# Last block of an SSD-and-MLP kernel: cross products one tile behind the squares, tile 14 by parts

## The chip, the cores and the metric

The kernel runs on one core of a Trainium2 chip. The metric is the device time of one execution in microseconds (us); a time of a kernel is the median of several executions.

## The reference

A selective state-space layer (mamba2's SSD) over 4 batches, 8 heads and 768 steps is followed by a two-layer perceptron with a hardswish between its layers. The output of the first, (4 x 768) tokens by 256, is the input `x` of the second:

```python
# SSD, chunk by chunk, per batch and head
y[:, :, sl] = einsum(CB * L, xc) + einsum(Cc, state) * decay_to_i
state = decay_full * state + sum_j(B_j x_j decay_from_j)
# MLP: 3072 tokens, 256 -> 2048 -> 256
h = x @ w_in
g = h * clip(h + 3, 0, 6) / 6
out = g @ w_out
```

All is in 32-bit floats. The change is in the MLP of the last block of tokens.

## The kernel before

The 768 steps are cut into six chunks of 128. Chunk k of all four batches gives one block of 512 tokens (four groups b of 128), and the MLP runs block by block. While the MLP of block k is computed, the SSD of the next chunk is woven into it. The order of instructions is written out by hand; each engine runs its own instructions in that order, and waits only for the data and buffers that it needs. The last block (k = 5) has no chunk after it.

**The first layer of a block** works on 16 tiles f of 128 hidden units by 512 tokens, each in a PSUM bank. The weights and the inputs were split into a high part, a low part and a `less` part, so that one-pass matmuls give the accuracy of 32-bit ones. `squares(k, f)` takes the tile's bank and runs four matmuls (high x high, low x low); `enlarge` scales the bank on ACT (L714); `cross` adds two more matmuls (less x less). All six are matmuls of L694, which writes `h`. `factor` then makes the hardswish: `ramp` on ACT (L733) reads `h` and writes `gT`, `times_ramp` on DVE (L738) multiplies it by `h`. After that the bank is free. In the last block four banks, `f0` to `f3`, take the tiles in turn, so tile f + 4 needs the bank of tile f.

**The second layer of the last block** is summed up in PSUM over the 16 tiles, with two running sums, `squares` (rows with `o`) and `cross` (rows with `o_less`). `split_g(k, f)` splits a tile of `gT` in the same way: the high part on ACT (L840), the low part and the `less` part on DVE (L841, L842), into buffers that four tiles share in turn. `split_out` has split `w_out` a quarter at a time (L812 on ACT, L815 and L822 on DVE), partly inside the loop of the last block. `last_out(k, f)` then runs, for each b, three one-pass products of 256 columns (L858): high, low, and `less`. Two tiles were not split: for 14 and 15 the function `whole` multiplies `gT` by `w_out` in 32 bits (L863), and each such product shows as two instructions of TensorE.

The last call of `last_out` ends the kernel: ACT scales the `squares` sums (L880), and for each b in the order 0, 2, 1, 3 come the last products, a DVE addition (L885) and the store of the result (L886) on SP's queue.

**Order around the change.** The block before (k = 4) ends with `wide_units`, with rows of L897, a DVE addition (L965) and a DVE transpose (L911). Shortly before its end, `lead` and `lead_on` run the squares of tiles 0 and 1 of the last block and enlarge them. The last block's loop goes over f = 2 to 15; in it a tile's `cross` and `factor` come two tiles behind the squares, `split_g` three behind, and `last_out` five behind.

Of the kernel before, what the change touches and what calls it, by code (L numbers as in the profile page):

```python
# [21 lines left out]
def kernel(  # L22
# [26 lines left out]
    NB, NH, S, D = x.shape  # L49
# [4 lines left out]
    NF = DF // P  # L54
# [636 lines left out]
    def part_products(k, f, n, m, start=False):  # L691
        w, y = w_parts[f // FP][n], y_parts[k][m]
        for j in range(NK):
            nc.tensor.matmul(  # L694
                out=hs_[k, f], lhsT=w[j][:, f % FP * P:(f % FP + 1) * P], rhs=y[:, j],
                start=(start and j == 0), stop=True, skip_group_check=True)

    def squares(k, f, low=True):

        pool, tag = ((ps, "f0"), (ps, "f1"), (ps, "f2"), (ps, "f3"), (ps_y, "y0"), (ps_y, "y1"))[  # L700
            f % (6 if k < NC - 1 else 4)]
        hs_[k, f] = pool.tile([P, TB], FP32, name="h", tag=tag)
        part_products(k, f, 0, 0, start=True)
        if low:
            part_products(k, f, 1, 1)

    def enlarge(k, f):

        h = hs_[k, f]
        if k < NC - 1 and (f < 2 if k == 1 else f % 4 == 3):  # L710
            nc.vector.tensor_scalar(
                out=h, in0=h, scalar1=1.0 / EPS + 1.0, scalar2=None, op0=ALU.mult)
        else:
            nc.scalar.activation(h, h, AF.Copy, scale=1.0 / EPS + 1.0)  # L714

    def cross(k, f):
        part_products(k, f, 2, 2)

    def factor(k, f):
        ramp(k, f, hs_[k, f])  # L720
        times_ramp(k, f, hs_[k, f])
# [9 lines left out]
    def ramp(k, f, h):  # L731

        nc.scalar.activation(  # L733
            gTs[k][:, f], h, AF.Relu, bias=half, scale=1.0 / 6.0)

    def times_ramp(k, f, h):
        g = gTs[k][:, f]
        nc.vector.scalar_tensor_tensor(  # L738
            out=g, in0=g, scalar=1.0, in1=h, op0=ALU.min, op1=ALU.mult)
# [89 lines left out]
    def g_homes():  # L829
        two = loads.tile([P, 2, 2, TB], F32R, name="g_pair", tag="raw", bufs=NRAW)  # L830
        ones = [pool.tile([P, 2, TB], F32R, name="g_pair", tag=tag, bufs=1)
                for pool, tag in ((const, f"w{NP - 1}"), (att, "yT"))]
        ends_["pair"] = ones + [two[:, 0], two[:, 1]]
        ends_["less"] = [pool.tile([P, TB], F32R, name="g_less", tag=tag, bufs=1)
                         for pool, tag in ((att, "bT"), (att, "csT"), (att, "bs"), (loads, "B"))]

    def split_g(k, f):
        g, pair, less = gTs[k][:, f], ends_["pair"][f % 4], ends_["less"][f % 4]
        hi, lo = pair[:, 0], pair[:, 1]
        nc.scalar.activation(hi, g, AF.Copy, scale=1.0 - EPS / 2)  # L840
        nc.vector.tensor_tensor(out=lo, in0=g, in1=hi.bitcast(FP32), op=ALU.subtract)  # L841
        nc.vector.scalar_tensor_tensor(  # L842
            out=less, in0=lo.bitcast(FP32), scalar=-1.0 / EPS, in1=hi.bitcast(FP32),
            op0=ALU.mult, op1=ALU.add)
        g_parts[f] = (hi, lo, less)

    def last_out(k, f):

        if f == 0:
            ends_["squares"] = [ps_o.tile([P, 2, DM], FP32, name="o", tag="o") for _ in range(2)]  # L850
            ends_["cross"] = [
                ps_y.tile([P, 2, DM], FP32, name="o_less", tag=f"y{u}") for u in range(2)]
            ends_["res"] = ffn.tile([P, NB, DM], FP32, name="res", tag="wide")
        o = [[ends_[n][b // 2][:, b % 2] for b in range(NB)] for n in ("squares", "cross")]

        def product(b, t, n):
            w = out_parts[t // FP][n][:, (t % FP) * DM:(t % FP + 1) * DM]
            nc.tensor.matmul(  # L858
                out=o[n // 2][b], lhsT=g_parts[t][n][:, b * P:(b + 1) * P], rhs=w,
                start=(t == 0 and b % 2 == 0 and n != 1), stop=True, skip_group_check=True)  # L860

        def whole(b, t):
            nc.tensor.matmul(  # L863
                out=o[1][b], lhsT=gTs[k][:, t, b * P:(b + 1) * P], rhs=w_out[:, t],
                start=False, stop=True, skip_group_check=True)

        if f < NF - 4:
            for b in range(NB):
                for n in range(3):
                    product(b, f, n)  # L870
            return
        for t, ns in ((f, range(2)), (f, (2,)), (NF - 2, ()), (f + 1, range(2))):
            for b in range(NB):
                for n in ns:
                    product(b, t, n)
                if not ns:
                    whole(b, t)
        res = ends_["res"]
        for u in range(2):
            nc.scalar.activation(  # L880
                res[:, 2 * u:2 * u + 2], ends_["squares"][u], AF.Copy, scale=1.0 / EPS + 1.0)
        for b in (0, 2, 1, 3):
            product(b, f + 1, 2)
            whole(b, NF - 1)
            nc.vector.tensor_tensor(out=res[:, b], in0=o[1][b], in1=res[:, b], op=ALU.add)  # L885
            nc.sync.dma_start(out=out[b * S + k * P:b * S + k * P + P, :], in_=res[:, b])  # L886
# [167 lines left out]
    for k in range(NC):  # L1054
# [53 lines left out]
            continue  # L1108
        if c == NC:
            g_homes()  # L1110
            for f in range(2, NF):
                squares(k, f)
                if f > 4:
                    last_out(k, f - 5)
                cross(k, f - 2)
                enlarge(k, f)
                factor(k, f - 2)
                if f > 2:
                    split_g(k, f - 3)
                if 3 <= f < 13:  # L1120
                    next(outs_[2 + f // 8])
            for f in (NF - 2, NF - 1):
                cross(k, f)
            factor(k, NF - 2)
            factor(k, NF - 1)
            split_g(k, NF - 3)
            for f in range(NF - 5, NF - 3):
                last_out(k, f)
            continue
        for f in range(2, NF):  # L1130
            squares(k, f)
# [95 lines left out]
```

## Time and profile before

| | |
|---|---|
| median of 3 runs | 343.51 us (343.08 to 343.96) |
| profiled execution | 343.9 us, of which 342.1 us are the span |
| TensorE (PE) | 334.7 us busy, 98% of the span |
| TensorE weight loads (PEld) | 266.1 us, 78% |
| VectorE (DVE) | 237.2 us, 69% |
| ScalarE (ACT) | 198.0 us, 58% |
| GpSimd (POOL) | 125.0 us, 37% |
| last block, from its first matmul | 293.5 us to the end |

The span goes from the first to the last instruction on the core. The busy share is an average over all stages, and overlapping matmuls count from their start to a modelled end, so the distance between starts says more than the length of a row. The chain that ended last is followed back from the last instruction, at each step to what released it. In rows, `x4` is a count of instructions, the first number is the start in us, the second the time that the group took, and a bracket names idle time before it and what ended that. The granted TensorE clock is 1.0 throughout.

### The profile page before, as it was taken

The page shows a single profiled execution, that of the slowest core. Times are in us where ns is not written, and L with a number is a line of the kernel's source. Part 1 is how long each engine was busy: PE and PEld are TensorE (multiplying, and loading weights), DVE is VectorE, ACT ScalarE, POOL GpSimd, SP SyncE. Part 2 cuts the span into 40 slices and gives each one's busy share as a digit, 9 for nine tenths or more (in the row PEclk, how much of TensorE's full clock was granted, in tenths as well). Part 3 has the DMA queues.
Part 4 walks back from the last instruction along what each step waited for, and adds up shares of the span by engine and source line. Part 5 has one row for each costly group of instructions (what it writes and reads, how often), then busy time and mean ns, then how long its engine had stood idle before and what let it go on. Part 6 is the DMA issues. An engine that isn't in the chain of part 4 may idle for free.

```text
span 342.1 us, 8181 instructions
## 1 busy us (share of the span) xinstructions
PE 334.7 (98%) x3332; PEld 266.1 (78%) x3332; DVE 237.2 (69%) x378; ACT 198.0 (58%) x415; POOL 125.0 (37%) x123
## 2 busy tenths in 40 slices
PE   6999999999999999999999999999999999999995
PEld 1664448888888888888888888888888888799994
DVE  6599999998399859565528555537476455498973
ACT  4759878757986480576460576470586030667661
POOL 3300000190284798089813089920079700000000
PEclk9999999999999999999999999999999999999999
DMA  8989968042590216166107276101160001110001
GB/s 172 175 301 192 196 216 196 2 54 75 141 136 1 60 32 147 27 85 68 24 12 154 35 90 63 23 3 17 31 77 2 2 2 17 30 17 2 1 2 61
DMA packets 89605, 25.15 MB, mean 74 GB/s; under 512 B 82208, under 2 KB 85952, under 8 KB 89056
## 3 DMA queue, kind: packets, MB, share of 16 engines
q1 hardware_dynamic: 85184, 23.33, 36.4%
q10 hardware_dynamic: 4384, 1.31, 1.8%
q8 instruction: 26, 0.43, 0.5%
q14 instruction: 11, 0.09, 0.1%
HBM read 21.33 MB, written 3.29 MB: 72 GB/s over the span
## 4 chain that ended last, share of the span: by engine, by line
PE 96%; DVE 2%; DMA 1%; ACT 0%; issue 0%; ACTq 0%
PE h L694 32%; PE wb L897 13%; PE wc L897 8%; PE o L751 8%; PE h L626 8%; PE wa L897 8%; PE o L858 4%; PE y L604 3%; PE y L503 2%; PE o_less L858 2%; PE cb L530 2%; PE y L544 1%; PE o_less L863 1%; PE d L357 1%; DMA pre<-in_a_dram 1%; PE d L493 1%
## 5 line engine op out<-in xcount | busy, mean ns | idle before, releaser
L738 DVE SCALAR_TENSOR_TENSOR gT<-gT,h 128x512 f32<-128x512 f32 x96 | 64.8, 685 | 35.9 <-ACT gT L733 34.4
L733 ACT ACTIVATE gT<-h,half 128x512 f32<-128x512 f32 x96 | 65.2, 685 | 23.9 <-PE h L694 21.9
L714 ACT ACTIVATE h<-h 128x512 f32<-128x512 f32 x66 | 38.2, 584 | 41.1 <-PE h L694 41.0
L694 PE MATMUL h<-y_hi,w_part 128*128 128x512 f32 x160 | 51.8, 408 | 0.2 <-DVE gT L738 0.2
L694 PE MATMUL h<-y_less,w_part 128*128 128x512 f32 x160 | 49.7, 397 | 0.0
L694 PE MATMUL h<-y_lo,w_part 128*128 128x512 f32 x160 | 49.5, 395 | 0.0
L797 POOL TENSOR_TENSOR s<-gT 128x512 f32<-128x512 f32 x16 | 23.8, 1489 | 46.5 <-DVE gT L738 46.5
L694 PEld LDWEIGHTS h<-y_lo,w_part 128*128 128x128 f32 x160 | 30.0, 188 | 7.4
L694 PEld LDWEIGHTS h<-y_hi,w_part 128*128 128x128 f32 x160 | 29.9, 188 | 7.2 <-DVE gT L738 0.8
L694 PEld LDWEIGHTS h<-y_less,w_part 128*128 128x128 f32 x160 | 29.3, 188 | 5.9
L385 ACT ACTIVATE L<-L,cum_n 128x64 f32<-128x64 f32 x128 | 31.6, 337 | 0.0
L751 PE MATMUL o<-w_out,gT 128*128 128x256 f32 x128 | 28.8, 381 | 0.0
L626 PE MATMUL h<-yT,w_in 128*128 128x512 f32 x64 | 27.7, 594 | 0.0
L751 PEld LDWEIGHTS o<-w_out,gT 128*128 128x128 f32 x128 | 24.1, 190 | 3.8 <-issue 0.5
L158 POOL TENSOR_SCALAR_AFFINE_SELECT L<-L 64x1024 f32<-64x1024 f32 (+1 forms) x16 | 20.3, 1276 | 11.6 <-DMA L<-cum_d 11.2
L574 DVE TENSOR_TENSOR L<-L,cb 128x512 f32<-128x512 f32 x24 | 15.2, 682 | 13.1 <-PE cb L530 13.1
L403 POOL TENSOR_TENSOR tmp<-state,eto 128x256 f32<-128x256 f32 x5 | 4.1, 817 | 54.2 <-ACT eto L389 54.1
L626 PEld LDWEIGHTS h<-yT,w_in 128*128 128x128 f32 x64 | 12.1, 190 | 14.9 <-issue 12.9
L797 POOL TENSOR_TENSOR s<-gT,s 128x512 f32<-128x512 f32 x16 | 21.3, 1338 | 0.9
L396 POOL TENSOR_TENSOR bs<-B,L 128x128 f32<-128x128 f32 x24 | 11.7, 501 | 26.9 <-ACT L L385 21.4
L797 POOL TENSOR_TENSOR gT<-gT 128x512 f32<-128x512 f32 x16 | 20.6, 1293 | 0.9
L797 POOL TENSOR_TENSOR s<-s,gT 128x512 f32<-128x512 f32 x16 | 20.5, 1287 | 0.0
(137 smaller groups left out, 594.2 us busy)
## 6 DMA issues: line engine op xcount, KB each, us to landing
raw<-in_moe_w_out_dram SPq DMA_DIRECT2D x4, 1024.0 KB
L<-cum_d SPq DMA_DIRECT2D x8, 512.0 KB
xt<-in_x_dram SPq DMA_DIRECT2D x6, 512.0 KB
raw<-in_moe_w_in_dram SPq DMA_DIRECT2D x3, 1024.0 KB
out_dram<-back SPq DMA_DIRECT2D x128, 16.0 KB
pairs<-in_C_dram SPq DMA_DIRECT2D x40, 32.0 KB
eto<-cum_e SPq DMA_DIRECT2D x20, 64.0 KB
B<-in_B_dram SPq DMA_DIRECT2D x5, 256.0 KB
```

Of the source, the lines that this page charges most:

```text
L158: nc.gpsimd.affine_select(out=t[rows], in_=t[rows], pattern=pattern, compare_op=ALU.is_ge, fill=-1e5, base=base, channel_multiplier=-1)
L385: nc.scalar.activation(Ls[c][:, b, h], Ls[c][:, b, h], AF.Exp, bias=cum_n[:, c, g:g + 1])
L574: nc.vector.tensor_tensor(out=Ls[c][:, :, hs], in0=Ls[c][:, :, hs], in1=cbs[c][q], op=ALU.mult)
L626: nc.tensor.matmul(out=h, lhsT=w_in[f // FP][:, j, f % FP * P:(f % FP + 1) * P], rhs=yTs[k][:, j].rearrange("p b i -> p (b i)"), start=(j ...
L694: nc.tensor.matmul(out=hs_[k, f], lhsT=w[j][:, f % FP * P:(f % FP + 1) * P], rhs=y[:, j], start=(start and j == 0), stop=True, skip_group_ ...
L714: nc.scalar.activation(h, h, AF.Copy, scale=1.0 / EPS + 1.0)
L733: nc.scalar.activation(gTs[k][:, f], h, AF.Relu, bias=half, scale=1.0 / 6.0)
L738: nc.vector.scalar_tensor_tensor(out=g, in0=g, scalar=1.0, in1=h, op0=ALU.min, op1=ALU.mult)
L751: nc.tensor.matmul(out=o[:, b % 2], lhsT=gTs[0][:, f, b * P:(b + 1) * P], rhs=w_out[:, f], start=(f == 0 and b % 2 == 0), stop=True, skip_ ...
L797: nc.gpsimd.tensor_tensor(out=o, in0=p_, in1=q_, op=op)
L858: nc.tensor.matmul(out=o[n // 2][b], lhsT=g_parts[t][n][:, b * P:(b + 1) * P], rhs=w, start=(t == 0 and b % 2 == 0 and n != 1), stop=True, ...
L897: nc.tensor.matmul(out=bank[:, slot], lhsT=lhs[:, j], rhs=rhs[:, j], start=(clear and j == 0), stop=True, skip_group_check=True)
```

## The change

The last block's loop gets another order. `cross` and `factor` of tiles 0 and 1 come ahead of the loop; in the loop, `cross` and `factor` come one tile behind the squares in place of two, and `split_g` two behind in place of three. The loop has one round more (f = 16), without squares, for the cross of tile 15. Tile 14 is now split like the others and multiplied by twelve one-pass products, and only tile 15 stays whole. The last call of `last_out` is for tile 13: it runs the squares products of tiles 13 and 14, then the `less` products of 13, and in its end loop the `less` product of 14 and the whole product of 15 for each b.

```diff
@@ last_out
-        if f < NF - 4:
-            for b in range(NB):
-                for n in range(3):
-                    product(b, f, n)
-            return
-        for t, ns in ((f, range(2)), (f, (2,)), (NF - 2, ()), (f + 1, range(2))):
+        for t, ns in ((f, range(3)),) if f < NF - 3 else (
+                (f, range(2)), (f + 1, range(2)), (f, (2,))):
             for b in range(NB):
                 for n in ns:
                     product(b, t, n)
-                if not ns:
-                    whole(b, t)
+        if f < NF - 3:
+            return
         res = ends_["res"]
@@ the last block
             g_homes()
-            for f in range(2, NF):
-                squares(k, f)
+            for f in range(2):
+                cross(k, f)
+                factor(k, f)
+            for f in range(2, NF + 1):
+                if f < NF:
+                    squares(k, f)
                 if f > 4:
                     last_out(k, f - 5)
-                cross(k, f - 2)
-                enlarge(k, f)
-                factor(k, f - 2)
                 if f > 2:
-                    split_g(k, f - 3)
+                    cross(k, f - 1)
+                if f < NF:
+                    enlarge(k, f)
+                if f > 2:
+                    factor(k, f - 1)
+                split_g(k, f - 2)
                 if 3 <= f < 13:
                     next(outs_[2 + f // 8])
-            for f in (NF - 2, NF - 1):
-                cross(k, f)
-            factor(k, NF - 2)
-            factor(k, NF - 1)
-            split_g(k, NF - 3)
-            for f in range(NF - 5, NF - 3):
-                last_out(k, f)
+            last_out(k, NF - 4)
+            last_out(k, NF - 3)
             continue
```

## The prediction

> **What bounds the kernel now.** I read the page first: its busy shares and its chain that ended last. Then I read that chain in order of time from 270 us on, and at two places where something other than TensorE stands in it I read the instructions by time, engine by engine.
>
> ```profile
> PE 334.7 (98%) x3332; PEld 266.1 (78%) x3332; DVE 237.2 (69%) x378; ACT 198.0 (58%) x415; POOL 125.0 (37%) x123
> PE 96%; DVE 2%; DMA 1%; ACT 0%; issue 0%; ACTq 0%
> ```
>
> TensorE is 96% of the chain, so only two things count: what work TensorE gets, and the few places where it stands still. The chain in order of time has two such places in the last block, one at its head and one at its end:
>
> ```profile
> 293.88 0.95 PE h L694 x4
> ...
> 294.92 0.41 ACT h L714
> ...
> 295.41 0.69 ACT gT L733
> ...
> 296.13 0.70 DVE gT L738
> ...
> 296.87 2.59 PE h L694 x10
> ...
> 306.64 1.40 PE h L694 x6
> 308.04 0.23 PE o L858 x2
> ...
> 309.46 1.40 PE h L694 x6
> ...
> 333.42 1.73 PE o_less L863 x8
> 335.15 0.95 PE o L858 x8
> ...
> 337.20 0.04 issue
> 337.24 0.39 PE o_less L858
> ```
>
> A tile in the steady part is six matmuls of L694 (1.40 us) and twelve products of L858: from 308.04 to 309.46, 1.42 us, so 0.118 us each. One tile is 2.82 us, and from 299 to 332 us TensorE never idles. The eight L863 instructions are four whole products (each runs as two): 1.73 us, 0.43 us a product. At the head the chain leaves TensorE for ACT and DVE. The TensorE rows of that place:
>
> ```profile
> 295.59 0.62 PE L694 MATMUL h<-y_lo,w_part 128*128 128x512 f32 x2
> 296.05 0.62 PE L694 MATMUL h<-y_less,w_part 128*128 128x512 f32 x2
> 296.87 0.73 PE L694 MATMUL h<-y_hi,w_part 128*128 128x512 f32 x2 [0.21 <-DVE gT L738]
> 297.44 0.62 PE L694 MATMUL h<-y_lo,w_part 128*128 128x512 f32 x2
> ```
>
> Pairs normally start 0.466 us apart (295.59, 296.05), so the pair at 296.87 should have started at 296.52: 0.35 us late. The next pair comes 0.57 us after it in place of 0.466, its weight load no longer running ahead: 0.10 more. The pair is tile 4's squares. With four banks it needs tile 0's bank, and that is free when the DVE step of tile 0 (L738, 296.13 to 296.82) has read it. The stall is 0.45 us.
>
> **The change, part by part.**
>
> *First two tiles' crosses ahead of all.* TensorE's order was squares 2, cross 0, squares 3, cross 1, squares 4; it becomes cross 0, cross 1, squares 2, squares 3, cross 2, squares 4. Cross 0 and 1 need only their enlargement, which ACT ran at 291.73 for 1.07 us, so until 292.80; the block begins at 293.53. Cross 0 starts there (a first pair takes 0.66 us, as now), and its ramp on ACT follows at about 294.4 and ends at 295.1. On DVE the new step stands behind the previous block's L965 and its transpose L911 (294.38, 0.71 us), so tile 0's L738 runs from 295.1 to 295.8. Squares 4 reach TensorE at 296.99. The bank is free 1.2 us ahead, and the 0.45 us go.
>
> What comes late next is cross 2, due at 296.52. Its enlargement stands behind two ramps on ACT now. Ramp 1 starts at 295.0 and ACT can take the next at 295.5. Squares 2, 0.466 us ahead of where squares 3 stood, end so that the enlargement starts at 295.79 (now tile 3's starts 1.13 us after its squares begin: 296.25 after 295.12) and ends at 296.37. With 0.04 us of handing on it makes 296.52, but the load, which normally leads by 0.23 us, starts about 0.1 us late. Between nothing and 0.1 us; I take 0.02, since the load led by only 0.10 when it had to (297.44 after 296.87). If the ramps pushed it further, the whole 0.45 us could return here. Cross 3 needs an enlargement that ends by 297.4 and is due at 297.92; cross 4, behind the two weight splits of L812 on ACT, one by 300.3 against 300.7.
>
> *Crosses one tile behind.* No instruction is added by this, and the six L694 matmuls of a step still follow each other (cross, then the next squares). Cross f-1 needs an enlargement from a step earlier, 2.82 us before. ACT's three instructions of a tile hold it 1.7 us (304.32 to 306.02; 2.7 in the two steps with L812), DVE's four at most 2.76; both were so before. Buffers of a split tile are reused four tiles on, and their last reader stays one whole step ahead. Cost: nothing, covered by a full step; without that cover each late cross would cost what it is late. No DMA is moved: the final stores stay where they are on SP's queue, and POOL does nothing here.
>
> *Fourteenth's cross at the end, fifteenth by parts.* (Counted as in the code, tiles 13 and 14.) Removed: four whole products of tile 14, 1.73 us. Added: twelve products, 12 x 0.118 = 1.42 us. Both are on the path: -0.31 us. Also added are one ACT step (L840, 0.63) and two DVE steps (L841, L842, 0.69 each) for tile 14, off the path if in time. To see that, set zero at the start of cross 14. In the trace, from the cross pair at 329.02: ramp 0.67 later, L738 at 1.40, L841 at 2.00, L842 at 2.79 to 3.48, the next L738 0.61 after a L842 starts. TensorE: cross 14 to 0.47, products of 11 to 1.89, cross 15 to 2.36, products of 12 to 3.78, squares products of 13 to 4.72, then those of 14; its first lo product is at 4.84. DVE: L842 of 13 to 3.48, L738 of 15 from 3.40, L841 of 14 from 4.00 to 4.69. That is 0.15 us ahead of its use, about what load and handing on take: between 0 and 0.1, I take 0. L842 of 14 ends at 5.48 for a use at 6.14, and tile 15's L738 at 4.09 for 6.26.
>
> *The end loop* keeps its 0.31 us stop at 337.24: b=1's product writes the tile that DVE's first L885 (336.76, 0.42 us) is still reading. The two ACT steps ahead of it now run beside tile 13's four crosses, 0.47 us more cover. That L885 waits for the whole product of b=0 too, whose second pass, at 336.28 for 0.38 us, ends at 336.66. So it can start at most 0.06 us sooner; I take 0.
>
> *A weight load for each product.* The twelve new products need twelve loads of 0.188 us; the four whole ones had eight. In the trace twelve products with twelve loads pass in 1.42 us, less than the 2.26 us of the loads alone, so they overlap. The Trainium skill, "TensorE: Matmul & The Clock Gate", Part 3, "The mechanism", says that a weight load overlaps running matmuls only where their row groups differ. All these fill the whole array, so by that rule they would not overlap. By the page's figures (an estimate: 107 ns a load, 109 ns a stream) the twelve would be 2.59 us and the sum +0.43 us; the trace's 1.42 us disagrees with the rule here.
>
> **Sum.** -0.45 + 0.02 - 0.31 = -0.74 us. The profiled execution took 343.9 us (span 342.1 and 1.8 around it), so 343.2 for such a one; it stands 0.4 above the median, and from the median of 343.51 the forecast is 342.8.
>
> **The rivals.**
> 1. *The stall moves to cross 2* (or tile 14's lo product): the ramps or L738 hold ACT or DVE longer than reckoned, the 0.45 us return, -0.31 remains: 343.2. For it: slacks of 0.1 us; one L842 in this block came 0.46 us late without any effect. Against: the durations are steady within 0.01. 0.18.
> 2. *The end loop's stop goes too.* The waits view gives the first L885's 1.7 us of idling to ACT's L880. Were ACT the true holder and L885 free 0.31 us earlier: -1.05, 342.5. Against: the matmul's end at 336.66. 0.06.
> 3. *Slower: the new products don't hide their loads.* In the tail parts of two tiles alternate; if the twelve ran as load after stream, 12 x (0.118 + 0.188) = 3.67 us for 1.73, with the stall gone +1.49: 345.0. It decides from 0.182 us a product ((1.73 + 0.45) / 12) on for any loss. Against: eight such products at 335.15 took 0.95. 0.05.
> 4. The forecast: 0.71. That the change does nothing is excluded: L863 must fall from 16 instructions to 8.
>
> **How the numbers follow.** 0.3% is 1.03 us, about what a measurement of this kernel can tell from no change. The forecast of -0.74 lies inside, 0.3 short of the bound. Three runs before spread over 0.88 us, so a difference of two medians is easily 0.35 to 0.5 off: rather over two in five of the forecast's share (0.31) fall beyond the bound, the rest within. Rival 2, just at the bound, gives 0.03 to faster, rival 1 0.02; rival 3, and 0.02 of scatter, go to slower: faster 0.36, same 0.57, slower 0.07. The range takes rival 2 less 0.35 of scatter, 342.1, and rival 1 with that scatter added, 343.5.
>
> **What would show it.** In the profile after: L863 x8 and L858 x180; no DVE releaser of L694 near 296.9, squares 4 starting near 297.0 and right behind cross 2; TensorE unbroken up to the last loop, with the products of tile 14 at 0.118 us; the stop of 0.3 us ahead of b=1 still there; span near 341.4. A wait of L694 for ACT's L714 near 296.5, or of L858 for L841 in the last 6 us, would prove rival 1; a product pitch above 0.18 us in the tail rival 3. A change anywhere before 293.5 us would be outside of this reckoning.

## The result, and the profile after

The changed kernel takes 342.81 us (median of 22 runs, 341.78 to 343.40) against 343.74 us for the kernel before (22 runs, 342.68 to 345.84): a ratio of 0.9972, 95% interval 0.9961 to 0.9983. By the ratio that is 0.96 us less, between 0.58 and 1.34. A second series (the first experiment below) gave 0.9966, 0.9953 to 0.9979. The profiled execution has a span of 340.0 us, 2.1 us less than before; most of that difference is not of the change, as will be seen.

The changed kernel is four lines shorter in `last_out`, so L885 of before is L881 now, and L880 is L876. From the page, the line of busy times and the first line of the chain:

```profile
PE 332.4 (98%) x3336; PEld 265.1 (78%) x3336; DVE 238.8 (70%) x380; ACT 198.6 (58%) x416; POOL 125.0 (37%) x123
...
PE 94%; DMA 3%; DVE 1%; SPq 1%; issue 0%; DVEq 0%
```

TensorE has four instructions more: twelve products came, eight of the whole ones went. DMA has 3% of the chain in place of 1%: here the chain leads back to the loads at the start of the kernel, by another way than before. The chain in order of time, in the last block:

```profile
292.55 5.63 PE h L694 x24
298.18 0.23 PE o L858 x2
...
331.58 1.90 PE o L858 x16
333.49 0.60 PE o_less L858 x5
334.09 0.43 PE o_less L863 x2
...
335.07 0.04 issue
335.11 0.39 PE o_less L858
...
336.51 0.42 DVE res L881
```

ACT and DVE no longer stand between the matmuls at the head: there are 24 of L694 in one piece. The wait of tile 4's squares for tile 0's bank (the bank wait) is gone. The sixteen squares products of tiles 13 and 14 pass at 0.119 us each. The stop ahead of b=1 is still there, at 335.07. In the waits view of the last block, the rows of TensorE and its weight loads are these two:

```profile
PEld o_less L858 <- DVE res L881: 0.4, 1, 0.4
PEld h L694 <- ACT h L714: 0.2, 1, 0.2
```

The second is new: cross 2 waits for its enlargement. In the instructions by time, the pair at 295.17 is cross 2, and the next pair (tile 4's squares) should have started 0.466 us behind it:

```profile
295.17 0.69 PE L694 MATMUL h<-y_less,w_part 128*128 128x512 f32 x2
295.70 0.63 PE L694 MATMUL h<-y_hi,w_part 128*128 128x512 f32 x2
```

It started 0.53 us behind: 0.06 us lost, where the bank wait had cost 0.45. There is a third place, which the prediction does not have. These are the first products of tile 0, in the trace of before and then in that of after:

```profile
299.30 0.40 PE L858 MATMUL o<-v_pair,g_pair 128*128 128x256 f32 x2
299.53 0.38 PE L858 MATMUL o_less<-v_less,g_less 128*128 128x256 f32 x1
299.75 0.40 PE L858 MATMUL o<-v_pair,g_pair 128*128 128x256 f32 x2
```

```profile
298.02 0.40 PE L858 MATMUL o<-v_pair,g_pair 128*128 128x256 f32 x2
298.25 0.28 PE L858 MATMUL o_less<-v_less,g_less 128*128 128x256 f32 x1
298.37 0.40 PE L858 MATMUL o<-v_pair,g_pair 128*128 128x256 f32 x2
```

From the first o_less product to the next pair it was 0.22 us and is 0.12. Before, tile 0's last split step on DVE was this:

```profile
298.78 0.69 DVE L842 SCALAR_TENSOR_TENSOR g_less<-g_pair 128x512 fp32r<-128x512 f32 x1
```

It ended at 299.47, 0.06 us ahead of its use. The product's weight load therefore started together with the product, at 299.53; after the change it starts at 298.14, 0.11 us ahead of its product.

Two measures serve in all that follows; the variants have one trace each, and two traces of the same kernel gave blocks within 0.02 us of each other. The **block** is the time from the last block's first L694 (293.53 us before, 292.20 after) to the start of the last addition on DVE (338.65 and 336.51). It was 45.12 us and is 44.31: 0.81 us less. The **lead** is the time from the first L626 to the block's first L694: 269.99 us before, 269.90 after, so nothing changed there. The rest of the 2.1 us stands ahead of the first L626, which started at 23.54 us before and at 22.30 after.

### The profile page after: what moved, and what is told of

Read it like the earlier page. It is cut to its first block, busy times and chain, and to the rows that moved or that the text cites. A ratio compares the mean times of both kernels' runs of the same rounds, so it can differ in the third digit from the quotient of the medians.

```text
span 340.0 us, 8193 instructions
## 1 busy us (share of the span) xinstructions
PE 332.4 (98%) x3336; PEld 265.1 (78%) x3336; DVE 238.8 (70%) x380; ACT 198.6 (58%) x416; POOL 125.0 (37%) x123
## 4 chain that ended last, share of the span: by engine, by line
PE 94%; DMA 3%; DVE 1%; SPq 1%; issue 0%; DVEq 0%
PE h L694 33%; PE wb L893 13%; PE wc L893 8%; PE o L751 8%; PE h L626 8%; PE wa L893 8%; PE o L858 4%; PE y L604 3%; PE o_less L858 2%; PE y L503 2%; PE cb L530 2%; DMA raw<-in_moe_w_in_dram 2%; PE y L544 1%; DMA pairs<-in_C_dram 1%; SPq L101 1%; PE o_less L863 1%
## 5 line engine op out<-in xcount | busy, mean ns | idle before, releaser
L738 DVE SCALAR_TENSOR_TENSOR gT<-gT,h 128x512 f32<-128x512 f32 x96 | 64.8, 685 | 33.7 <-ACT gT L733 32.2
L733 ACT ACTIVATE gT<-h,half 128x512 f32<-128x512 f32 x96 | 65.1, 684 | 25.7 <-PE h L694 23.7
L714 ACT ACTIVATE h<-h 128x512 f32<-128x512 f32 x66 | 38.2, 585 | 39.0 <-PE h L694 38.7
L694 PE MATMUL h<-y_hi,w_part 128*128 128x512 f32 x160 | 51.5, 407 | 0.0
L694 PE MATMUL h<-y_less,w_part 128*128 128x512 f32 x160 | 50.1, 399 | 0.0
L694 PE MATMUL h<-y_lo,w_part 128*128 128x512 f32 x160 | 49.5, 395 | 0.0
L694 PEld LDWEIGHTS h<-y_lo,w_part 128*128 128x128 f32 x160 | 30.0, 188 | 7.4
L694 PEld LDWEIGHTS h<-y_hi,w_part 128*128 128x128 f32 x160 | 30.0, 188 | 6.7 <-DVE gT L738 0.2
L694 PEld LDWEIGHTS h<-y_less,w_part 128*128 128x128 f32 x160 | 29.2, 188 | 6.0 <-ACT h L714 0.2
L626 PE MATMUL h<-yT,w_in 128*128 128x512 f32 x64 | 27.7, 594 | 0.0
L626 PEld LDWEIGHTS h<-yT,w_in 128*128 128x128 f32 x64 | 12.1, 190 | 14.9 <-issue 13.2
L858 PE MATMUL o<-v_pair,g_pair 128*128 128x256 f32 x120 | 21.1, 281 | 0.0
```

The source lines that it names most:

```text
L626: nc.tensor.matmul(out=h, lhsT=w_in[f // FP][:, j, f % FP * P:(f % FP + 1) * P], rhs=yTs[k][:, j].rearrange("p b i -> p (b i)"), start=(j ...
L694: nc.tensor.matmul(out=hs_[k, f], lhsT=w[j][:, f % FP * P:(f % FP + 1) * P], rhs=y[:, j], start=(start and j == 0), stop=True, skip_group_ ...
L733: nc.scalar.activation(gTs[k][:, f], h, AF.Relu, bias=half, scale=1.0 / 6.0)
L738: nc.vector.scalar_tensor_tensor(out=g, in0=g, scalar=1.0, in1=h, op0=ALU.min, op1=ALU.mult)
L858: nc.tensor.matmul(out=o[n // 2][b], lhsT=g_parts[t][n][:, b * P:(b + 1) * P], rhs=w, start=(t == 0 and b % 2 == 0 and n != 1), stop=True, ...
```

## The experiments

Each was timed in alternation with the kernel before; the ratio is against that.

**The changed kernel again** (no edit).

> The changed kernel once more. Theory: the change acts only in the last block, by three amounts: the bank stall at its head goes (0.45 us, of which a late cross 2 gives 0.06 back), the wait of the first o_less product for tile 0's L842 goes (0.10), and the tail has 0.31 us less TensorE work; in all 0.80 us less, ratio about 0.9977. The first matmul of the last block starts somewhere between 292 and 294 us, as in any run of either kernel, since the loads at the start end at different times. Rival: the block's start 1.33 us earlier in the first profile belongs to the change: then the block starts near 292.2 us here and in every variant that has the new order, and the ratio is near 0.994.

Measured: ratio 0.9966 (0.9953 to 0.9979). Block 44.33 us, 0.79 less than before. The block starts at 292.63, the first L626 at 22.61. Over the twelve traces of this study the first L626 starts anywhere from 22.30 to 24.61 us, and the lead is 269.8 to 270.1 us in all of them. The latest starts (24.61 and 23.68) belong to variants with the new order, and two variants with the old one, but for two early crosses, started at 22.57 and 22.82. So the 1.24 us at the start are not of the change. Two things vary there. The matmuls of L316 shortly ahead of it start at 17.66 to 17.97 us in ten traces; in the two whose chain begins with the load `pre` (before, and one late) they start at 18.90 and 19.25. And in eight traces TensorE stops for 0.32 to 1.24 us inside the matmuls of L604. The profile names no releaser for that stop, and its cause stays open.

**The kernel before again**, for its trace.

> The kernel before once more, for its trace. Theory: the block is 45.12 us long again, with the same three stops (0.45 us ahead of tile 4's squares, 0.10 ahead of the first o_less product, 0.31 ahead of b=1), and starts somewhere between 292 and 294 us, as far behind the first L626 (269.9 us) as in every other run. Rival: the block's start near 293.5 us belongs to this kernel.

Measured: block 45.10 us, with the bank wait at 296.94 as at 296.87 the first time. The block starts at 293.60, the first L626 at 23.52; on these two traces alone the rival would stand, and it falls by the variants' starts named above. The two equal starts came about in different ways: here the stop inside L604 took 1.14 us, and the first time there was none. The same program against itself came out at 0.9977 (0.9953 to 1.0002): the timing scatters by nearly as much as the whole effect. That is why the block in the traces, which repeats within 0.02 us, has to carry the detail.

**Order only:** the new loop, tile 14 whole as before.

```diff
-                split_g(k, f - 2)
+                if f < NF:
+                    split_g(k, f - 2)
...
-            last_out(k, NF - 4)
-            last_out(k, NF - 3)
+            last_out(k, NF - 4)      # last_out as before the change
```

> The new order (first two crosses ahead, cross one tile behind), but tile 14 multiplied whole as before. Theory: the head's 0.39 and 0.10 us are gained, the tail's 0.31 is not: 0.49 us less than before, ratio 0.9986, and L863 still 16 instructions. From the last block's first L694 to the first L885 of the end, 0.5 us less than in the first profile of before. Rival (the tail makes the gain): no difference, ratio 1.000.

Measured: ratio 0.9992 (0.9976 to 1.0008), block 44.60 us, 0.52 less than before. The waits are the same two as after the change. So the order gives 0.52 us (0.49 reckoned), and the parts on top of it 0.28 (44.60 to 44.32; 0.31 reckoned). The ratio alone could not tell this from no change.

**Parts only:** the old loop, tile 14 by parts.

```diff
             split_g(k, NF - 3)
-            for f in range(NF - 5, NF - 3):
+            split_g(k, NF - 2)
+            for f in range(NF - 5, NF - 2):
                 last_out(k, f)           # last_out as changed
```

> The old order (cross two tiles behind), but tile 14 by parts at the end. Theory: without the earlier crosses the parts come too late. By the rows of before, L841 of tile 13 ends at 334.30 for a use at 333.38 (0.96 us stop) and L841 of tile 14 at 335.70 for a use at 335.29 (0.45 us stop); less 0.31 us of work this is 1.1 us slower than before, ratio 1.003, with TensorE's L858 waiting for DVE's L841 twice. Rival (the two parts of the change are independent, and the parts give 0.31 by themselves): 0.31 us faster, ratio 0.999, no such wait.

Measured: ratio 1.0030 (1.0019 to 1.0041), slower by 0.3%; block 46.37 us, 1.25 more than before. From the waits view:

```profile
PEld o L858 <- DVE g_pair L841: 0.8, 2, 0.4
PEld h L694 <- DVE gT L738: 0.6, 1, 0.6
...
PEld o_less L858 <- DVE g_less L842: 0.5, 1, 0.5
```

The two waits for L841 are at the places expected. The third line is one that I had not reckoned with: in the changed `last_out` tile 12's products run high, low and less for each b, so its first less product comes 0.7 us sooner than when all four b had their squares first. It costs 0.57 us, and since TensorE is that much later, the first wait for L841 makes it only 0.39 us late in place of 0.96. That the sum came out near the 1.1 expected is in part luck. The bank wait (second line) is still there, as in the kernel before. One half of the change alone costs more than both together gain.

**Two crosses ahead only:** all else as before.

```diff
+            for f in range(2):
+                cross(k, f)
+                factor(k, f)
             for f in range(2, NF):
...
-                cross(k, f - 2)
+                if f > 3:
+                    cross(k, f - 2)
```

(`factor` likewise.)

> Only the first two tiles' cross and factor ahead of the loop; all other crosses two tiles behind and tile 14 whole as before. Theory: the stall at the head is that of the first two tiles alone, so it goes without the closer order: 0.45 and 0.10 us less, and no late cross 2, 0.55 us less than before, ratio 0.9984, no idle time of L694 in the last block. Rival (the closer order removes the stall): the bank wait stays or moves to tile 5 or 6, ratio 1.000.

Measured: ratio 0.9993 (0.9979 to 1.0007), block 44.94 us: 0.18 less than before, not 0.55. The bank wait is gone, but the first products of tile 0 are now these:

```profile
297.93 0.40 PE L858 MATMUL o<-v_pair,g_pair 128*128 128x256 f32 x2
298.43 0.39 PE L858 MATMUL o_less<-v_less,g_less 128*128 128x256 f32 x1
```

0.50 us from pair to o_less product in place of 0.23. TensorE arrives sooner, and tile 0's split arrives no sooner: its L840 on ACT stands behind the enlargement of tile 3. Its DVE step L842 ends at 298.38, 0.05 us ahead of the product. So 0.37 us of the 0.55 are lost at the next place (0.27 late, 0.10 for the load). My theory, that the stall is one of the first two tiles alone, is wrong.

**The same, with every split one step earlier:**

```diff
-                if f > 2:
-                    split_g(k, f - 3)
+                split_g(k, f - 2)
...
-            split_g(k, NF - 3)
```

> As the kernel with only the first two crosses ahead, but every tile's split of g one step earlier (split_g two tiles behind, as in the change); crosses stay two tiles behind and tile 14 whole. There the first o_less product of the second layer still came about 0.37 us late, behind tile 0's L842, and the block was 0.18 us shorter than before. Theory: that wait is of the late split alone. Moved a step earlier it goes, and the block (from its first L694 to the last L885) is 0.55 us shorter than before, 44.57 us in place of 45.12, ratio 0.9984. Rival: the wait comes from DVE's load and needs the closer crosses: block 44.9 us, ratio 0.9993.

Measured: ratio 1.0188 (1.0175 to 1.0201), 6.5 us slower; block 51.64 us. Tile 0's products run unbroken here (298.34 to 299.77, 1.43 us), so the reading of the wait was right and the cure was wrong. ACT's instructions by time, in the steady part:

```profile
304.75 0.67 ACT L733 ACTIVATE gT<-h,half 128x512 f32<-128x512 f32 x1
307.01 0.63 ACT L840 ACTIVATE g_pair<-gT 128x512 fp32r<-128x512 f32 x1 [1.59 <-DVE gT L738]
307.55 0.58 ACT L714 ACTIVATE h<-h 128x512 f32<-128x512 f32 x1
```

The split of a tile (L840 at 307.01) now stands right behind the ramp of the same tile (L733 at 304.75), and needs the DVE step L738 that comes after that ramp. On DVE that step stands behind the previous tile's split and a step of `w_out`, and runs from 306.30 to 306.98. ACT idles 1.59 us meanwhile, and the next enlargement waits behind L840. The crosses come late by that, then the ramps and the banks: in the waits view the weight loads of L694 wait for L738 ten times, 7.0 us in all. All splits can move up only if cross and factor move up with them. That is what the closer crosses of the change allow.

**Two splits early:** the two crosses ahead as above, and of the splits only those of tiles 0 and 1 one step sooner.

```diff
-                if f > 2:
-                    split_g(k, f - 3)
+                if f != 4:
+                    split_g(k, f - 2 if f < 4 else f - 3)
```

> The kernel with only the first two crosses ahead, and of the splits of g only those of tiles 0 and 1 one step earlier; from tile 2 on three tiles behind as before. Theory: the kernel with all splits earlier lost its 6.5 us because each L840 then stood on ACT right behind the ramp whose L738 it needs, with the next enlargement behind it; tiles 0 and 1 are finished ahead of the loop and need no such wait. So the late first o_less product goes and nothing is lost later: block 44.57 us, 0.55 us less than before, ratio 0.9984. Rival: any split moved up delays an enlargement: block above 45 us.

Measured: ratio 0.9982 (0.9963 to 1.0001), block 44.81 us, 0.31 less than before, 0.24 more than expected. Tile 0's products run unbroken, and then comes this:

```profile
299.19 0.63 PE L694 MATMUL h<-y_less,w_part 128*128 128x512 f32 x2
299.82 0.73 PE L694 MATMUL h<-y_hi,w_part 128*128 128x512 f32 x2
```

The pairs are 0.63 us apart in place of 0.47, and it is 0.57 to the one after: 0.26 us lost. And the waits view names the bank again (L694 for L738, 0.4 us by the load), now tile 6's squares waiting for tile 2. With the crosses two behind, freeing the first places uncovers the next; with them one behind, only the 0.06 us of cross 2 remain.

**The end loop:** the changed kernel with the `less` products of tile 13, then with those of tiles 11, 12 and 13, moved into it.

```diff
-        for t, ns in ((f, range(3)),) if f < NF - 3 else (
-                (f, range(2)), (f + 1, range(2)), (f, (2,))):
+        late = (NF - 3,)      # second kernel: (NF - 5, NF - 4, NF - 3)
+        for t, ns in ((f, range(2 if f in late else 3)),) if f < NF - 3 else (
+                (f, range(2)), (f + 1, range(2))):
...
         for b in (0, 2, 1, 3):
+            for t in late:
+                product(b, t, 2)
             product(b, f + 1, 2)
```

> The changed kernel with the less products of tile 13 moved into the end loop, one per b. Theory: the stop of 0.31 us ahead of b=1 is what TensorE's work for b=2 (0.55 us) leaves uncovered of DVE's first addition; 0.12 us more work per b cuts it to 0.19 us, the block to 44.2 us (44.31 in the changed kernel). Rival: the stop follows the addition at a fixed distance, or the L880 copies become the late ones: block 44.3 us or more.

Measured for one tile: block 44.20 us, as the theory had it; ratio 0.9970 (0.9956 to 0.9984). From the chain in order of time:

```profile
336.76 0.43 PE o_less L863 x2
337.20 0.43 PE o_less L858 x2
337.62 0.43 PE o_less L863 x2
```

The two products of b=1 take 0.43 us where two take 0.23 elsewhere in the loop: the stop is 0.20 us now. By the trace it beats the changed kernel by 0.11 us and the one before by 0.92; the timings cannot tell it from the changed kernel.

> The same with the less products of tiles 11, 12 and 13 in the end loop, 0.35 us more per b. Theory: nothing of the 0.31 us is left, the block is 44.0 us, and against before 1.1 us less, ratio 0.9968. Rival: block 44.3 us as in the changed kernel, ratio 0.9977.

Measured for three tiles: ratio 1.0006 (0.9990 to 1.0023), block 44.96 us, 0.65 more than the changed kernel. The stop ahead of b=1 is gone, and a larger one came. TensorE's instructions by time:

```profile
331.00 2.18 PE L858 MATMUL o<-v_pair,g_pair 128*128 128x256 f32 x17
333.87 1.10 PE L858 MATMUL o<-v_pair,g_pair 128*128 128x256 f32 x7 [0.69 <-DVE g_pair L841]
```

The DVE step for which the second row waits is this, from the chain in order of time:

```profile
333.21 0.61 DVE g_pair L841
```

Eight products (0.94 us) no longer stand ahead of tile 14's, so TensorE comes to tile 14's low part that much sooner. Seventeen products from 331.00 end at 333.0; L841 ends at 333.82, and the next product starts at 333.87. That is 0.87 us late, and the lost lead of the load costs another 0.1; the stop that went gives 0.31 back. The slack of 0.15 us that the prediction gave tile 14's split is real, and the move spends it six times over.

**Tile 4's squares sooner:** the kernel with three late tiles, and tile 4's squares ahead of tile 2's cross.

> The previous one with tile 4's squares ahead of tile 2's cross. Theory: the 0.06 us for which cross 2 waits for its enlargement (L714) go too, as there is 0.93 us of other work in between: block 43.95 us, against before 1.17 us less, ratio 0.9966, and no wait of L694 in the last block. Rival: tile 4's squares then wait for their bank as before the change, 0.3 us or more.

```diff
-                if f < NF:
-                    squares(k, f)
+                if f < NF and f != 4:
+                    squares(k, f)
+                if f == 3:
+                    squares(k, 4)
```

Measured: ratio 0.9998 (0.9980 to 1.0016), block 45.14 us, 0.18 more than the kernel it was built on, not 0.06 less. The wait of cross 2 is gone. But cross 2 ends 0.9 us later for it, and so does tile 2's ramp; behind that on ACT come the two splits of L812 and tile 4's enlargement. That ended at 300.34, and cross 4, due at 300.22, started at 300.39; the pair after it came 0.57 us later, 0.10 more than without a wait. The slack of cross 4 was 0.68 us in the changed kernel (298.75 to 299.43; the prediction had 0.4). The move put the enlargement back by 0.74 us (from 5.96 to 6.70 us into the block) and brought TensorE there 0.08 us sooner.

## Why the prediction was right, and where it was not

The forecast was 342.8 us and 0.74 us less than before; measured are 342.81 and 0.96 less (0.58 to 1.34), and 0.80 by the traces of the block. That the time itself was met so closely is partly luck. The forecast starts from the median of three runs, 343.51, which is 0.23 us below that of the 22, and its difference is 0.22 us smaller than the measured one; the two nearly cancel. The difference, and each term in the traces, is the fairer test:

- **The stall at the head.** Reckoned at 0.45 us with 0.02 given back at cross 2; found at 0.45 and 0.06. The enlargement started 2.30 us after the block's first matmul, reckoned 2.26, and the load of cross 2 led by 0.04 us in place of 0.23. The range of 0 to 0.1 held it. The prediction named a wait of L694 for L714 near this place as proof of rival 1, under which the whole 0.45 us would return. The wait is there (0.2 us by the load), and rival 1 did not come true: the sign was too coarse, for most of that wait is lead that the load gave up.
- **The work at the tail.** Reckoned at 0.31 us less; the block with the new order goes from 44.60 to 44.32 us when tile 14 is done by parts. That hangs on products at 0.118 us, half of the 0.233 us that one of 512 columns takes, so nothing of a load shows. Sixteen products with their sixteen loads passed in 1.91 us at the end, and rival 3 is out. The Trainium skill, "TensorE: Matmul & The Clock Gate", Part 3, "The mechanism", has a rule by which a weight load overlaps running matmuls only of other row groups. By that rule alone the new products would have been a loss, and the trace disagrees with it here too. The same section of the Trainium skill also lets a load into a background weight buffer run ahead. No run here shows which buffer these loads go to.
- **Tile 14's split in time.** Reckoned 0.15 us ahead of its use. These are the rows after:

```profile
331.42 2.07 PE L858 MATMUL o<-v_pair,g_pair 128*128 128x256 f32 x16
331.63 0.68 DVE L841 TENSOR_TENSOR g_pair<-gT,g_pair 128x512 fp32r<-128x512 f32 x1
```

L841 ended at 332.31 for the tenth product, due at 332.49 (331.42 and nine of 0.119): 0.18 us ahead. Three tiles' `less` products in the end loop showed what it costs once that is spent.

- **The end loop's stop.** Reckoned as unchanged at 0.31 us. It is 0.30, and the rival that had ACT as the true holder is out by these rows after the change:

```profile
333.05 1.08 ACT L876 ACTIVATE res<-o 128x512 f32<-128x512 f32 x2 [1.65 <-PE o L858]
334.63 0.97 DVE L881 TENSOR_TENSOR res<-o_less,res 128x256 f32<-128x256 f32 x2 [1.52 <-PE o_less L863]
```

L876 ended at 334.13, 0.50 us ahead of the first addition (0.01 us before the change), and the addition came no sooner after the whole product of b=0: 0.70 us after its start, both times.

- **"Crosses one tile behind: cost nothing."** The cost was right, but the prediction gave the whole 0.45 us to the first two crosses. Those alone bring 0.18, since 0.37 us are lost at the next place; with two early splits they bring 0.31. The rest needs the closer crosses, without which the later splits cannot move up either. No run has the closer crosses without the first two ahead.
- **Missed:** the 0.10 us ahead of the first o_less product. The prediction says that TensorE never idles from 299 to 332 us, and it went by idle brackets. This late load shows no bracket on the matmul; the 0.22 us between rows show it. With the 0.04 us more at cross 2 this term makes the difference between 0.74 and 0.80.

The further 0.16 us between the traces and the timed ratio are inside its interval. The start, which differs by up to 2.3 us from trace to trace, could hold them; that is not shown.

## What to carry to other kernels

Where one engine is nearly the whole chain, its time can be summed from the distances between its starts, stops included. A short stop (0.06, 0.10 and 0.26 us here) shows only in those distances.

A stop that is freed moves TensorE ahead, and the next place with less slack than that becomes the stop. So reckon the new due time of every later step, not only of the one that was freed.

A step that is moved up on an engine with a fixed order needs inputs that are ready by then. Where L840 was put right behind the ramp of its own tile, it held up everything behind it, and the block grew by 6.5 us.

## What the runs showed of the hardware that was not expected

- A wait of a matmul falls on its weight load, which otherwise leads by 0.23 us (512 columns) or 0.11 us (256 columns). Once the lead is lost, the wait costs about 0.10 us on top of the lateness: behind a late pair of L694 the next came after 0.57 us in place of 0.466, before the change and in the variants alike.
- The first L626 starts between 22.30 and 24.61 us over these twelve traces, by the way of the first loads and by a stop of up to 1.24 us inside L604 that has no releaser in the profile. From there to the last block they agree within 0.3 us (269.8 to 270.1). A difference of spans of 2 us between two traces can lie wholly in the start.
